# A layer-norm, state-space and MLP kernel on one core: one ScalarE table set loaded by name, and a skip term moved from diagonal matmuls to elementwise ops

## Chip, cores and metric

One core of a Trainium2 chip. The metric is device time in microseconds (us) of one execution; lower is better. The profiled execution has a span (first to last instruction), which is 1.7 to 2.1 us shorter than the device time.

A run more than 1.5% above the fastest run of the same kernel is called slow and left out of ratios. A ratio is the mean time of a kernel's fast runs over the mean of the fast runs of the kernel before in the same rounds, so it is not quite the ratio of the medians that are quoted beside it.

## The reference, cut to what matters

```python
xn = layernorm(x)                                  # x: 2048 tokens of 448
s  = 2*Re(C h) + xn*Dskip                          # h: complex recurrence over the tokens
g  = silu(gelu(layernorm(xn) @ w1 + b1) @ w2 + b2) # 448 -> 1792 -> 448
out = x + s*g
```

The kernel works on 4 groups of 512 tokens, each two blocks of 256, and splits a block into even and odd tokens ("par" 0 and 1). The recurrence runs on pairs of tokens. Even tokens get `xn*Dskip` inside a precomputed matrix M0. For odd tokens the skip term is the subject of half of this change.

## The kernel before

Every operation is a task with an engine, the data it reads and writes, and a place in a fixed list, `ORDER`. That list was made beforehand by a planner. Each engine runs its tasks strictly in that order. Some tasks can run on either of two engines; `SECOND` lists those that take their second choice.

The parts that matter:

```python
# a warming activation: it makes ScalarE load a table set early
act(lambda e: e.activation(sgn[0:1, 3:4], sgn[0:1, 2:3], ACT.Ln, scale=-1.0), ["sgn"], ["warm"], ...)
...
ld("pool", b2bc[:], dram_ap(B_b2, 0, [[0, 128], [1, D]]), ["b2bc"], ..., reads=["sgn3"])   # sgn3 waits for "warm"
...
def first_norm():            # the first 128 even and 128 odd tokens, ahead of everything
    for par in range(2):
        ... bn_stats, bn_aggr on VectorE
        kb.add("act", [lambda e: e.activation(r1, var, ACT.Ln, ...),
                       lambda e: e.activation(r1, r1, ACT.Exp, scale=-0.5)], ..., chain=True)   # 1/sqrt(var)
        ... scale on VectorE, transpose on PE, copy on VectorE
...
def mm1_half(j, b, k3, prio):  # x @ w1 for one block of group 0: 8 matmuls, then gelu on ScalarE
    ...                        # needs the half (or both halves) of w1 that its columns lie in
...
def ym(g, b, par, prio):       # the output of one tile of 128 tokens
    ... 7 matmuls of h against CZ or CQ
    if par == 0: ... 4 matmuls xnT x M0
    else:        # odd tokens: xn * Dskip as matmuls against diagonal matrices Do
        fns += [lambda e: e.matmul(psum[:, bk, a:z], xnT[:, gx, 3 + i, xs], Do[:, i, ...], start=False, ...) for i, a, z in cuts]
    dve: t3 = psum * g_sb ;  dve: o_sb = t3 + x
```

## Time and profile before

| | before |
|---|---|
| device time, median | 165.68 us |
| first dense matmul (`mm1_half`, line L694) | 10.48 us |
| end of `mm1_half`, start of `mm2` | 25.67 us |
| PE idle from then to the last M0 matmul, which ends at 158.98 | 0 |
| table loads on ScalarE | 10 |

The page of the profile gives busy time, share of the span and instructions of each engine. Then come the granted PE clock in 40 equal slices (a digit is tenths of full speed) and the engines on the chain that ended last, that is, on the chain of work and waits that leads to the last instruction. PE is TensorE's matmuls and PEld its weight loads; DVE is VectorE, ACT ScalarE, POOL GpSimd; SP (SyncE) issues most transfers. A q behind a name means the queue that issues for that engine.

```profile
PE 155.3 (95%) x977; PEld 100.3 (61%) x977; DVE 124.5 (76%) x251; ACT 98.8 (60%) x156; POOL 33.4 (20%) x115
...
PEclk9955999999999999999999999999999999999999
...
PE 91%; ACT 3%; DVE 2%; DMA 1%; issue 1%; DVEq 0%
```

PE, the matmul engine, is the bound. The two fives in the clock row are a stretch at half speed. It begins at 8.82 and ends at 15.65 us, just where the dense matmuls start.

The timeline shows the head. Columns are start, duration, engine, source line, operation, output<-input, shape, count, and in brackets the idle time before it with what ended it.

```profile
3.81 0.29 ACT L368 ACTIVATE lnw<-lnmv,eps 128x1 f32<-128x1 f32 x1
4.12 1.28 ACT L369 ACT_TABLE_LOAD   x1
...
5.41 0.20 ACT L369 ACTIVATE lnw<-lnw 128x1 f32<-128x1 f32 x1
...
5.63 1.28 ACT L368 ACT_TABLE_LOAD   x1
...
6.93 0.29 ACT L368 ACTIVATE lnw<-lnmv,eps 128x1 f32<-128x1 f32 x1
...
7.24 1.28 ACT L369 ACT_TABLE_LOAD   x1
...
8.54 0.20 ACT L369 ACTIVATE lnw<-lnw 128x1 f32<-128x1 f32 x1
...
9.31 0.61 PE L374 MATMUL psum<-ident,xn_sb 128*128 128x128 bf16 x4 [2.81 <-DVE xn_sb L371]
...
10.48 7.04 PE L694 MATMUL psum<-xn2T,w_sb 128*128 128x256 bf16 x40 [0.56 <-issue]
```

Ln and Exp alternate, and each finds the other's table set loaded. Three loads of 1.28 us lie in series before the first dense matmul, and PE waits 2.81 us for them. The 40 matmuls that follow take 7.04 us because most of them run at half clock.

The second half of w1 is also on its way.

Issued at 3.7 and 4.2, w1's second half is complete at 12.06. Before, PE gets that far only at about 15.6, so it hurts nobody.

The diagonal matmuls show on the chain of waits (start, duration, what):

```profile
93.77 0.20 PE psum L739 x4
```

### The profile page before, as it was taken

What the parts mean: (1) busy time and instruction counts of PE and PEld (TensorE: products, weight loads), DVE (VectorE), ACT (ScalarE), POOL (GpSimd) and SP (SyncE); (2) the same over time, 40 slices, a digit from 0 to 9 for tenths busy, and PEclk for the clock granted to TensorE, in tenths of its full rate; (3) what the DMA queues carried; (4) which work ended last, traced back from release to release, by engine and by line L of the source; (5) the groups of instructions that cost most, each with busy time, mean ns of one, the idle gap of its engine ahead of it and who ended that gap; (6) DMA issues with size and microseconds to landing.
All of it is one profiled execution on the core that took longest, in us unless ns stands there. A gap on an engine that the chain in (4) does not pass through costs nothing.

```text
span 164.2 us, 2747 instructions
## 1 busy us (share of the span) xinstructions
PE 155.3 (95%) x977; PEld 100.3 (61%) x977; DVE 124.5 (76%) x251; ACT 98.8 (60%) x156; POOL 33.4 (20%) x115
## 2 busy tenths in 40 slices
PE   5559999999999999999999999999999999999991
PEld 5447996566766765555555555566667675555560
DVE  5175798976499988899996969732499489988953
ACT  4997979987958599965544480452158953360200
POOL 5227795400000580000205420000002300000000
PEclk9955999999999999999999999999999999999999
DMA  4999966899874006400000056402050000010021
GB/s 93 341 273 390 242 68 139 181 166 176 165 147 116 0 0 126 113 4 0 0 0 0 2 127 116 112 0 56 4 168 0 0 4 0 0 58 0 31 85 58
DMA packets 29880, 14.61 MB, mean 89 GB/s; under 512 B 24581, under 2 KB 29577, under 8 KB 29866
## 3 DMA queue, kind: packets, MB, share of 16 engines
q1 hardware_dynamic: 29810, 14.31, 37.2%
q0 software_dynamic: 48, 0.11, 0.5%
q8 instruction: 8, 0.13, 0.3%
q14 instruction: 6, 0.05, 0.1%
q10 hardware_dynamic: 8, 0.00, 0.0%
HBM read 6.77 MB, written 1.84 MB: 52 GB/s over the span
## 4 chain that ended last, share of the span: by engine, by line
PE 91%; ACT 3%; DVE 2%; DMA 1%; issue 1%; DVEq 0%
PE psum L709 26%; PE psum L678 22%; PE psum L608 13%; PE psum L730 12%; PE psum L694 9%; PE psum L733 4%; PE psum L597 3%; ACT L369 2%; DMA x_all<-in_A_x_dram 1%; PE psum L739 1%; DVE t L743 1%; ACT L368 1%; DVE tmp L745 1%; DVE lnst L366 0%; PE psum L374 0%
## 5 line engine op out<-in xcount | busy, mean ns | idle before, releaser
L709 PE MATMUL psum<-w_sb,gT 128*128 128x448 bf16 x224 | 44.2, 352 | 0.0
L678 PE MATMUL psum<-xn2T,w_sb 128*128 128x512 bf16 x168 | 38.6, 379 | 0.0
L709 PEld LDWEIGHTS psum<-w_sb,gT 128*128 128x128 bf16 x224 | 21.8, 98 | 19.3
L685 ACT ACTIVATE gT<-psum 128x1024 bf16<-128x1024 f32 x21 | 21.5, 1023 | 15.0 <-PE psum L678 13.3
L678 PEld LDWEIGHTS psum<-xn2T,w_sb 128*128 128x128 bf16 x168 | 21.6, 132 | 12.5 <-issue 0.2
L608 PE MATMUL psum<-xnT,BT 128*128 128x256 bf16 x196 | 24.0, 273 | 0.0
L608 PEld LDWEIGHTS psum<-xnT,BT 128*128 128x128 bf16 x196 | 19.0, 98 | 4.7 <-issue 0.3
L743 DVE TENSOR_TENSOR t<-psum,g_sb 128x448 bf16<-128x448 f32 (+2 forms) x17 | 10.1, 594 | 10.7 <-PE psum L733 8.6
L713 ACT ACTIVATE th<-o 128x448 f32<-128x448 f32 x16 | 8.8, 571 | 11.9 <-DVE o L712 11.8
L694 PE MATMUL psum<-xn2T,w_sb 128*128 128x256 bf16 x112 | 15.1, 304 | 0.6 <-issue 0.6
L633 DVE TENSOR_TENSOR_SCAN s_f<-cw,cur,v_sb 128x256 f32<-128x256 f32 x21 | 14.7, 735 | 0.3
L694 PEld LDWEIGHTS psum<-xn2T,w_sb 128*128 128x128 bf16 x112 | 13.3, 137 | 2.1 <-issue 0.8
L712 DVE TENSOR_TENSOR o<-psum,b2bc 128x448 f32<-128x448 f32 x16 | 9.8, 622 | 4.8 <-PE psum L709 4.7
L612 ACT ACTIVATE u_sb<-psum 128x512 bf16<-128x512 f32 x12 | 7.1, 595 | 9.9 <-PE psum L608 9.9
L730 PE MATMUL psum<-CQ,h_sb 128*128 128x448 bf16 (+2 forms) x63 | 12.0, 332 | 0.0
L730 PE MATMUL psum<-CZ,h_sb 128*128 128x448 bf16 x56 | 11.9, 352 | 0.0
L417 ACT ACTIVATE xn_sb<-x_all,lnw 128x448 bf16<-128x448 bf16 x16 | 11.4, 749 | 0.1
L714 DVE SCALAR_TENSOR_TENSOR g_sb<-th,o 128x448 bf16<-128x448 f32 x16 | 9.8, 619 | 1.8 <-ACT th L713 1.7
L701 ACT ACTIVATE gT<-psum 128x512 bf16<-128x512 f32 x14 | 8.2, 592 | 1.9 <-PE psum L694 1.7
L730 PEld LDWEIGHTS psum<-CQ,h_sb 128*128 128x128 bf16 x63 | 6.0, 98 | 4.2
L352 DVE BATCH_NORM_STATS2 lnst<-x_all 128x6 f32<-128x448 bf16 x14 | 8.3, 603 | 0.0
L730 PEld LDWEIGHTS psum<-CZ,h_sb 128*128 128x128 bf16 x56 | 5.4, 98 | 4.6
(151 smaller groups left out, 197.0 us busy)
## 6 DMA issues: line engine op xcount, KB each, us to landing
w_sb<-in_B_w_dram SPq DMA_DIRECT2D x2, 784.0 KB, 9.5
out_dram<-tmp SPq DMA_DIRECT2D x7, 224.0 KB, 2.2
w_sb<-in_B_w_dram SPq DMA_DIRECT2D x2, 672.0 KB, 6.2
x_all<-in_A_x_dram SPq DMA_DIRECT2D x3, 448.0 KB, 3.8
gT<-in_A_C_re_dram SPq DMA_DIRECT2D x1, 392.0 KB, 12.6
Bn<-in_A_B_re_dram SPq DMA_DIRECT2D x1, 336.0 KB, 8.3
Bn<-in_A_B_im_dram SPq DMA_DIRECT2D x1, 336.0 KB, 8.3
gT<-in_A_C_im_dram SPq DMA_DIRECT2D x1, 336.0 KB, 3.7
```

What stands on the lines that cost most here:

```text
L417: ("act", lambda e: e.activation(dst, src, ACT.Identity, bias=nb, scale=rs), 0.75, 0.2)]
L608: fns = [lambda e, r=r, m=m, d=d: e.matmul(psum[:, 4, r * NK:(r + 1) * NK], BT[:, m, d, :], xnT[:, gx, d, :], start=(d == 0), stop=(d == 6 ...
L633: dve(lambda e, i=i, ri=ri, init=init: e.tensor_tensor_scan(s_f[:, i, ri, :], col(R2, i).to_broadcast([128, NK]), v_sb[:, i, ri, :], init, ...
L678: fns = [lambda e, k=k, d=d: e.matmul(psum[:, b0 + k, :], w1_sb[:, d, fcol(2 * j + k)], rhs[:, d, :, :], start=(d == 0), stop=(d == 3)) fo ...
L685: act(lambda e: e.activation(gT[:, gb, 2 * j:2 * j + 2, :], psum[:, b0:b0 + 2, :], ACT.Gelu_apprx_tanh), [f"ps{b0}", f"ps{b0 + 1}"] + (WK ...
L694: fns = [lambda e, k=k, d=d: e.matmul(psum[:, banks[k], :].rearrange("p (r c) -> p r c", r=2)[:, :, cs], w1_sb[:, d, fcol(2 * j + k)], rhs ...
L709: fns = [lambda e, fi=fi: e.matmul(psum[:, bk, 0:D], gT[:, gb, fi, q * 128:(q + 1) * 128], w2_sb[:, fi, :], start=(fi == 0), stop=(fi == N ...
L712: dve(lambda e: e.tensor_tensor(o2[:, fb, :], psum[:, bk, 0:D], b2bc[:], ALU.add), [f"ps{bk}", "b2bc"], [f"oo{fb}"], 0.62, prio - 76)
L713: act(lambda e: e.activation(th[:, fb, :], o2[:, fb, :], ACT.Tanh, scale=0.5), [f"oo{fb}"] + (WK + WKP if g == 0 else []), [f"th{fb}"], 0. ...
L714: dve(lambda e: e.scalar_tensor_tensor(out=g_sb[:, gs, :], in0=th[:, fb, :], scalar=1.0, in1=o2[:, fb, :], op0=ALU.add, op1=ALU.mult), [f" ...
L730: fns = [lambda e, k=k: e.matmul(psum[:, bk, c0:c1], h_sb[:, hb, k, k0:k0 + 128], cm[:, k, c0:c1], start=(k == 0), stop=False) for k in ra ...
L743: dve(lambda e: e.tensor_tensor(t3[:, fb, c0:c1], psum[:, bk, c0:c1], g_sb[:, gs, c0:c1], ALU.mult), [f"ps{bk}", f"g{gs}"], [f"t3{fb}_{c0} ...
```

## The change

Its intent is twofold. One load of the table set that holds both ln and exp should replace the loads between them. The skip of odd tokens should leave PE, the bound, for engines with idle time. The new residual `xr = x + g*(xn*Dskip/2)` takes three elementwise ops per odd tile, each on GpSimd or VectorE. (The g in it is the kernel's `g_sb`, which holds twice the g of the reference; hence the half.)

```diff
-            act(lambda e: e.activation(sgn[0:1, 3:4], sgn[0:1, 2:3], ACT.Ln, scale=-1.0), ["sgn"], ["warm"], 0.2, 4 * PINNED, "exp")
+            act(lambda e: e.preload_act_table_set("natural_log_exp_and_others"), [], ["warm"], 0.05, 5 * PINNED, "exp")
...
-            pool(lambda e: e.memset(sgn[:, 3:4], math.pi / 2), ["warm"], ["sgn3"], 0.1, S0)
+            pool(lambda e: e.memset(sgn[:, 3:4], math.pi / 2), ["sgn"], ["sgn3"], 0.1, S0)
...
             ld("pool", b2bc[:], dram_ap(B_b2, 0, [[0, 128], [1, D]]), ["b2bc"], 114688, -50, reads=["sgn3"])
+            ld("pool", dbc[:], dram_ap(A_Dskip, 0, [[0, 128], [1, D]]), ["dbc"], 114688, -20, reads=["b2bc"])
+            pool(lambda e: e.tensor_scalar(dbc[:], dbc[:], 0.5, None, op0=ALU.mult), ["dbc"], ["dbc"], 0.8, -20)
...
+            def skip(g, b, prio):
...
+                for o, i0, i1, op, rd, wr, d1 in ((xd[:, b, :], xn_sb[:, b, D:896], dbc[:], ALU.mult, [f"xn{b}", "dbc"], f"xd{b}", 0.35),
+                                                  (xr[:, b, :], xd[:, b, :], g_sb[:, gs, :], ALU.mult, [f"xd{b}", f"g{gs}"], f"xr{b}", 0.55),
+                                                  (xr[:, b, :], xo, xr[:, b, :], ALU.add, [f"xr{b}"] + xk(2 * g + b), f"xr{b}", 0.55)):
+                    kb.either(("pool", ...), ("dve", ...), rd, [wr], prio)
...
-                        fns += [lambda e, i=i, a=a, z=z: e.matmul(psum[:, bk, a:z], xnT[:, gx, 3 + i, xs], Do[...], ...) for i, a, z in cuts]
+                        fns[-1] = lambda e: e.matmul(psum[:, bk, c0:c1], h_sb[:, hb, 6, k0:k0 + 128], cm[:, 6, c0:c1], start=False, stop=True)
...
+                    res = xr[:, b, c0:c1] if par else x_all[:, 2 * g + b, 0, c0:c1]        # xr is f32
```

`ORDER` and `SECOND` were planned anew (cut here).

## The prediction

> What bounds the kernel now. The chain of waits is 91% PE: a head of 10.48 us, then PE without a gap until 158.99, then about 5 us of VectorE drain and last store. So only three things move the time: when the dense matmuls start and at which clock, how much PE work there is, and whether another engine becomes late.
>
> Head (timeline, chain). The first norm's Ln, Exp, Ln, Exp on ScalarE pays a table load of 1.28 us at 4.12, 5.63 and 7.24, all three on the chain. The Trainium skill ("ScalarE: Activation LUTs", table sets) says natural_log_exp_and_others holds both functions, and about 1283 ns per load; the trace shows 1283 ns. PE waits 2.8 us for this, and the windows view shows the granted clock at 0.5 from 8.8 to 15.65.
>
> After: one load, over before x lands (2.90 and 3.43). The second row is normalised at about 5.5; mm1 could start at 6.9. It then meets a new limit, the weights: the first half of w1 lands at 6.4 (its 64-row rest 7.05), the second at 11.5 (rest 12.06). So mm1 starts at 7.1 rather than 10.5, runs three groups (24 matmuls) to about 9.9, then waits for w1's second half until about 11.8. Clock: the cold stretch was two 3.41-us windows after a half idle one ("TensorE: Matmul & The Clock Gate", Part 1; the trace agrees: 0.5 for 6.8 us) and cost 2.5 us. With a shorter gap I expect none at first, but the wait for w1 may bring one cold window (1.7 us). The half-block mm1, now ending at 25.84, should end at 21.9 (warm) to 23.6 (one cold window): 2.2 to 3.9 us gained, not the 3.85 of the loads one for one.
>
> PE work. The diagonal matmuls are 0.20 us per odd tile, 8 tiles: 1.6 us, all on the chain.
>
> Moved and added. Of 24 tensor ops of 128x448 the order puts 9 on VectorE and 15 on GpSimd. By traced ops of that shape (0.39 bf16, 0.62 with f32) VectorE gets 4.8 us, and 1.7 from the final add reading f32; it loses 5 diagonal builds (1.2): 124.5 to about 129 us. GpSimd gets about 20 us (33 to 53), at an estimated 1.3 us each, with idle time to spare. ScalarE loses 5 loads. VectorE was 16.6 of 17 us busy between 71 and 88 us, so it is the likeliest new limit; I allow 0.8 us of new PE gaps. The last adds with f32 cost 0.1 us; their xr should be ready about 1.5 us ahead.
>
> Sum: 165.7 - 3.2 (head) - 1.6 + 0.8 + 0.1 = 161.8; as the order was planned anew, with transposes of B and C earlier, I shade it to 161.5 us, range 159.8 to 163.9. Chances: faster by over 2% 0.67, within 2% 0.31, slower 0.02.
>
> What would show it: table loads 10 to 5, none between Ln and Exp; mm1's first matmul at about 7.1; a PE gap of 1 to 2 us near 10 to 12 ended by the DMA of w1; cold clock for 0 or 3.4 us rather than 6.8; no Do matmuls; the chain about 91% PE still; VectorE about 129 us busy.
>
> What would make it wrong: a longer cold clock around the w1 wait, so that the head gains under 2; GpSimd and VectorE slowing each other, so that xr or h comes late and PE gets gaps from 70 to 110; GpSimd ops far above 1.3 us; or w1 landing earlier than before, 1 to 2 us more.

## More of the kernel before

In the view of DMA issues from 3.5 to 4.5 us the columns are the transfer, the issuing queue, the count, the size, and the time from issue to landing.

```profile
w_sb<-in_B_w_dram SPq DMA_DIRECT2D x1, 672.0 KB, 7.8
b2bc<-in_B_b_dram POOLq DMA_DIRECT2D x1, 112.0 KB, 6.4
w_sb<-in_B_w_dram SPq DMA_DIRECT2D x1, 112.0 KB, 7.9
```

## The result, and the profile after

| | before | after |
|---|---|---|
| device time, median | 165.68 us | 160.97 us |
| ratio, 95% interval | | 0.9719 (0.9703 to 0.9736) |
| first dense matmul | 10.48 | 7.45 |
| start of `mm2` | 25.67 | 20.80 |
| PE gaps after that | 0 | 0.95 us |
| end of the last M0 matmul | 158.98 | 153.93 |
| span | 164.2 | 159.4 |

The time fell within the range, 0.5 us below the forecast. Where it came from, in the spans: 4.87 us up to the start of `mm2` (25.67 - 20.80), 0.18 from there to the last M0 matmul (133.31 - 133.13), and 0.25 given back in the drain (5.22 to 5.47). That makes 4.80.

The page of the kernel after, the same three lines:

```profile
PE 151.2 (95%) x944; PEld 97.3 (61%) x944; DVE 132.8 (83%) x254; ACT 92.6 (58%) x152; POOL 56.6 (36%) x132
...
PEclk9999999999999999999999999999999999999999
...
PE 72%; DMA 10%; SPq 4%; DVE 4%; POOL 4%; ACT 2%; issue 1%; DVEq 0%; ACTq 0%; POOLq 0%
```

The cold stretch is gone. PE is still busy 95% of the span but holds only 72% of the chain: something else got in. The head, in the timeline:

```profile
2.16 1.28 ACT L283 ACT_TABLE_LOAD   x1 [2.16 <-issue]
...
3.85 0.29 ACT L373 ACTIVATE lnw<-lnmv,eps 128x1 f32<-128x1 f32 x1 [0.41 <-DVE lnmv L372]
4.18 0.20 ACT L374 ACTIVATE lnw<-lnw 128x1 f32<-128x1 f32 x1
...
4.52 0.29 ACT L373 ACTIVATE lnw<-lnmv,eps 128x1 f32<-128x1 f32 x1
...
4.85 0.20 ACT L374 ACTIVATE lnw<-lnw 128x1 f32<-128x1 f32 x1
...
7.45 2.80 PE L699 MATMUL psum<-xn2T,w_sb 128*128 128x256 bf16 x24 [1.22 <-DMA w_sb<-in_B_w_dram]
...
10.72 1.93 PE L699 MATMUL psum<-xn2T,w_sb 128*128 128x256 bf16 x16 [0.46 <-issue]
```

No load stands between Ln and Exp, and both rows are scaled 3.7 us sooner (4.85 against 8.54). The brackets now name the new limit: the first 24 matmuls wait for w1's first half. PE then stops for 0.46 us, until w1's second half has landed at 10.63. That half came 1.4 us sooner than before (view of DMA issues, kernel after, 3.5 to 4.5 us; b2's load is no longer in that view):

```profile
w_sb<-in_B_w_dram SPq DMA_DIRECT2D x1, 672.0 KB, 6.4
w_sb<-in_B_w_dram SPq DMA_DIRECT2D x1, 112.0 KB, 6.4
```

What took PE's share of the chain is in the chain of waits from 27 us on (start, duration, what):

```profile
27.00 3.99 DMA dbc<-in_A_Dskip_dram
...
31.08 1.49 POOL dbc L338
...
32.72 1.04 POOL xd L730
...
33.86 1.02 DVE xn_sb L421
...
34.91 0.55 ACT xn_sb L422
...
35.58 0.56 ACT th L718
36.14 0.49 ACT u_sb L617
...
36.87 1.70 PE psum L613 x14
```

`dbc`, the skip weights, is loaded only after b2 has landed and after GpSimd's norm work. It lands at 31.0 and is halved. The first `xd` then reads `xn_sb`, and the next group's norm can overwrite `xn_sb` only after that. That norm stands on VectorE and ScalarE in front of `th` and `u_sb`, and `u_sb` frees the PSUM bank that PE needs. The totals of that stretch (20 to 46 us, view of waits: who waited for whom, total us, times, longest):

```profile
POOL dbc L338 <- DMA dbc<-in_A_Dskip_dram: 3.4, 1, 3.4
...
DVE xn_sb L421 <- POOL xd L730: 1.3, 1, 1.3
...
PE psum L613 <- ACT u_sb L617: 1.0, 2, 0.5
```

### The profile page after: what moved, and what is told of

Read it like the earlier page. It is cut to its first block, busy times and chain, and to the rows that moved or that the text cites. A ratio compares the mean times of both kernels' runs of the same rounds, so it can differ in the third digit from the quotient of the medians.

```text
span 159.4 us, 2700 instructions
## 1 busy us (share of the span) xinstructions
PE 151.2 (95%) x944; PEld 97.3 (61%) x944; DVE 132.8 (83%) x254; ACT 92.6 (58%) x152; POOL 56.6 (36%) x132
## 3 DMA queue, kind: packets, MB, share of 16 engines
HBM read 6.89 MB, written 1.84 MB: 55 GB/s over the span
## 4 chain that ended last, share of the span: by engine, by line
PE 72%; DMA 10%; SPq 4%; DVE 4%; POOL 4%; ACT 2%; issue 1%; DVEq 0%; ACTq 0%; POOLq 0%
PE psum L683 21%; PE psum L714 20%; PE psum L613 12%; PE psum L746 12%; DMA x_all<-in_A_x_dram 7%; SPq L84 4%; PE psum L749 4%; PE psum L602 3%; DMA dbc<-in_A_Dskip_dram 3%; DVE lnst L357 1%; POOL lnw L400 1%; POOL dbc L338 1%; DVE t L755 1%; PE psum L752 1%; POOL xd L730 1%
## 5 line engine op out<-in xcount | busy, mean ns | idle before, releaser
L683 PE MATMUL psum<-xn2T,w_sb 128*128 128x512 bf16 x168 | 38.1, 379 | 0.0
L683 PEld LDWEIGHTS psum<-xn2T,w_sb 128*128 128x128 bf16 x168 | 21.8, 132 | 12.9 <-issue 0.2
L690 ACT ACTIVATE gT<-psum 128x1024 bf16<-128x1024 f32 x21 | 21.5, 1023 | 11.8 <-PE psum L683 11.6
L719 DVE SCALAR_TENSOR_TENSOR g_sb<-th,o 128x448 bf16<-128x448 f32 x16 | 10.9, 682 | 4.4 <-ACT th L718 4.4
L699 PE MATMUL psum<-xn2T,w_sb 128*128 128x256 bf16 x112 | 12.8, 273 | 1.7 <-DMA w_sb<-in_B_w_dram 1.2
L699 PEld LDWEIGHTS psum<-xn2T,w_sb 128*128 128x128 bf16 x112 | 12.1, 132 | 2.0 <-DMA w_sb<-in_B_b_dram 1.4
L730 POOL TENSOR_TENSOR xr<-xd,g_sb 128x448 f32<-128x448 bf16 x4 | 4.5, 1119 | 24.8 <-DVE g_sb L719 20.9
L421 DVE TENSOR_SCALAR xn_sb<-x_all,lnw 128x448 bf16<-128x448 bf16 x20 | 10.3, 531 | 2.0 <-POOL xd L730 1.3
L746 PE MATMUL psum<-CQ,h_sb 128*128 128x448 bf16 (+2 forms) x54 | 10.5, 332 | 0.0
L422 ACT ACTIVATE xn_sb<-x_all,lnw 128x448 bf16<-128x448 bf16 x10 | 7.5, 755 | 4.4 <-DVE xn_sb L421 3.4
```

The source lines that it names most:

```text
L421: on = [("dve", lambda e: e.tensor_scalar(dst, src, rs, nb, op0=ALU.mult, op1=ALU.add), 0.4, 0.12), ("act", lambda e: e.activation(dst, sr ...
L683: fns = [lambda e, k=k, d=d: e.matmul(psum[:, b0 + k, :], w1_sb[:, d, fcol(2 * j + k)], rhs[:, d, :, :], start=(d == 0), stop=(d == 3)) fo ...
L690: act(lambda e: e.activation(gT[:, gb, 2 * j:2 * j + 2, :], psum[:, b0:b0 + 2, :], ACT.Gelu_apprx_tanh), [f"ps{b0}", f"ps{b0 + 1}"] + (WK ...
L699: fns = [lambda e, k=k, d=d: e.matmul(psum[:, banks[k], :].rearrange("p (r c) -> p r c", r=2)[:, :, cs], w1_sb[:, d, fcol(2 * j + k)], rhs ...
L719: dve(lambda e: e.scalar_tensor_tensor(out=g_sb[:, gs, :], in0=th[:, fb, :], scalar=1.0, in1=o2[:, fb, :], op0=ALU.add, op1=ALU.mult), [f" ...
L746: fns = [lambda e, k=k: e.matmul(psum[:, bk, c0:c1], h_sb[:, hb, k, k0:k0 + 128], cm[:, k, c0:c1], start=(k == 0), stop=False) for k in ra ...
```

## The experiments

They ran in three sets, each on another chip and with its own 7 runs of the kernel before, to which its ratios refer. Every time in the table is a median of 4 runs. Results were correct except where a wrong result is announced.

| run | median us (range) | ratio to before (95%) | `mm2` starts | PE gaps after it |
|---|---|---|---|---|
| before | 165.68 (165.54 to 165.7) | | 25.67 | 0 |
| after | 160.97 (160.87 to 161.19) | 0.972 | 20.80 | 0.95 |
| set 1: tab_only | 164.19 (163.17 to 165.92, slow) | 0.992 (0.985 to 0.999) | 22.50 | 0.28 |
| tab_b2bc | 164.74 (163.56 to 165.49) | 0.995 (0.990 to 1.000) | 22.20 | 2.07 |
| nodiag_only (wrong result) | 164.35 (163.95 to 164.49) | 0.993 (0.991 to 0.995) | 25.75 | 0 |
| after_oldtab | 166.42 (166.37 to 167.07) | 1.007 (1.005 to 1.009) | 24.76 | 2.58 |
| set 2: after_again | 161.86 (161.52 to 162.53) | 0.979 (0.977 to 0.982) | 21.52 | 0.64 |
| after_b2bc_early | 165.84 (164.59 to 166.44) | 1.002 (0.997 to 1.008) | 25.43 | 0.52 |
| after_dbc_early | 160.62 (160.12 to 161.68) | 0.972 (0.968 to 0.976) | 22.28 | 0.13 |
| after_skip_tiny (wrong result) | 161.0 (160.61 to 161.42) | 0.974 (0.971 to 0.976) | 21.62 | 0.46 |
| set 3: after_control | 161.52 (160.63 to 164.03, slow) | 0.974 (0.970 to 0.978) | 20.44 | 1.84 |
| tab_b2bc_mid | 161.83 (161.21 to 162.67) | 0.978 (0.974 to 0.982) | 21.24 | 0 |
| after_skip_dve | 161.33 (160.03 to 164.11, slow) | 0.973 (0.965 to 0.981) | 20.38 | 0.90 |
| dbc_warm | 161.34 (160.8 to 161.71) | 0.974 (0.972 to 0.977) | 21.69 | 0 |

The last two columns come from the one profiled execution, which need not be the median one. That matters for the kernels with an early start. Gaps under 0.1 us are left out.

### tab_only: the table set alone, in the old order

```diff
 # kernel before
-act(lambda e: e.activation(sgn[0:1, 3:4], sgn[0:1, 2:3], ACT.Ln, scale=-1.0), ...)
+act(lambda e: e.preload_act_table_set("natural_log_exp_and_others"), [], ["warm"], ...)
```

> The kernel before with one edit, the warming Ln replaced by the load of the set that holds ln and exp. Theory (the head is worth its table loads, up to the next limit, which is w1's second half): the dense matmuls start at 7.3 to 7.5 us instead of 10.48, pause from about 10.2 until w1's second half lands at about 12, no cold clock or one window, the half-block mm1 ends at 22.2 to 23.9 instead of 25.84, time 162.0 to 163.7 us. Rival (the old order was planned for a late start, so the transposes of B, which landed at 30 to 31, take the gain back as PE gaps near 30): 164 us or more, with gaps there.

Timeline of PE, kernel tab_only:

```profile
7.73 2.83 PE L694 MATMUL psum<-xn2T,w_sb 128*128 128x256 bf16 x24 [0.63 <-DVE xn2T L376]
12.43 1.93 PE L694 MATMUL psum<-xn2T,w_sb 128*128 128x256 bf16 x16 [1.87 <-DMA w_sb<-in_B_w_dram]
```

The head did what the theory said: an early start, then a pause of 1.87 us until w1's second half had landed, at 12.34. The times fall into two groups: 163.17 and 163.19, then 165.2 and 165.92. The mean granted clock of the runs was 0.996 and 1.0 in the first group, 0.99 in both of the second. One 3.4-us window at half clock would lower the mean by 0.01 (an estimate: 1.7 of 162 us). The profile of after_b2bc_early, which has just one such window, shows a mean of 0.990. So the second group looks like the cold window that the prediction feared after the pause. No profile fell on such a run, so this is argued, not shown. Only the quicker two lie in the theory's range of 162.0 to 163.7. The ratio of 0.992 mixes the groups (165.2 counts as fast); the quicker two alone give 0.986. The old order made only 0.28 us of new gaps; the rival's gaps near 30 were not there.

### tab_b2bc: with b2's load behind the parameter work, in the old order

```diff
 # tab_only; ORDER: the task that loads b2bc moved behind GpSimd's last-but-two parameter ops
```

> The same, and the load of b2 is moved in GpSimd's order behind its parameter work, as in the changed kernel. Theory (b2's broadcast load on the early queues is what held w1's second half back to 12.06 before and its absence let it land at 10.63 after): w1's second half lands at about 10.6, mm1's pause shrinks to about 0.5 us, the half-block mm1 ends at about 20.8, time 1.2 to 1.5 us below the run with the table alone. Rival (w1 landed earlier for another reason): same as the run with the table alone within 0.3 us.

w1's second half landed at 10.62, as expected. The run still was no faster than tab_only, for two reasons that its profile shows. The clock came up only at 11.14 (the trace's first record of full clock), so the first groups of `mm1_half` ran cold: 40 matmuls took 6.09 us without a pause. And b2 now landed too late, at 27.84, for its first reader. View of waits, kernel tab_b2bc, 25 to 42 us:

```profile
DVE o L717 <- DMA b2bc<-in_B_b_dram: 3.7, 1, 3.7
```

VectorE was held 3.7 us, and PE got 2.07 us of gaps. The experiment confounded two things, so tab_b2bc_mid repeated it later.

### nodiag_only: the diagonal matmuls taken out, nothing in their place

```diff
 # kernel before, wrong result on purpose
-fns += [lambda e, i=i, a=a, z=z: e.matmul(psum[:, bk, a:z], xnT[...], Do[...], ...) for i, a, z in cuts]
+fns[-1] = lambda e: e.matmul(psum[:, bk, c0:c1], h_sb[:, hb, 6, ...], cm[:, 6, c0:c1], start=False, stop=True)
```

> The kernel before without the diagonal matmuls of the odd tokens and with nothing in their place: WRONG RESULT on purpose. Theory (PE is the bound throughout, so their 8 x 0.2 us come off one for one): 164.0 to 164.3 us, ratio about 0.990 to 0.992. Rival (they hide under weight loads or other waits): 165.2 us or more.

From the start of `mm2` to the last M0 matmul it took 131.91 us instead of 133.31: 1.40, which is seven tiles of 0.20. The eighth tile ends behind the last M0 matmul, where the chain has passed to VectorE, and its 0.2 gains nothing. In device time the gain was 1.1 us by the medians, 1.2 by the ratio. So PE is the bound, as the theory says, but the term was 1.2 to 1.4, not 1.6.

### after_oldtab: the changed kernel with the old warming

```diff
 # kernel after
-act(lambda e: e.preload_act_table_set("natural_log_exp_and_others"), [], ["warm"], ...)
+act(lambda e: e.activation(cwk[0:1, 0, 0:1], sgn[0:1, 0:1], ACT.Ln, scale=-1.0), ["sgn"], ["warm", "cwk", "cwk3"], ...)
```

> The changed kernel with the old way of warming (an Ln on ScalarE before the norm), so that the loads come back between Ln and Exp. Theory: the dense matmuls start at about 10.5 again, the clock goes cold for 6.8 us again, the half-block mm1 ends at about 25.8; the new PE gaps of 0.95 us near 36 to 41 vanish, because PE comes later to them; time 164.3 to 165.3 us. Rival (the new order and the GpSimd work carry a good part of the gain): below 163.5 us.

It was slower than expected, and slower than the kernel before. Two lines of the timeline of PE, kernel after_oldtab:

```profile
10.45 6.11 PE L699 MATMUL psum<-xn2T,w_sb 128*128 128x256 bf16 x40 [0.56 <-issue]
...
120.93 1.94 PE L683 MATMUL psum<-xn2T,w_sb 128*128 128x512 bf16 x8 [1.27 <-DMA xn2T<-xn_sb]
```

The start went back to 10.45. The new order could not use a late start: b2 landed at 29.87 and `dbc` at 34.12. PE had gaps of 1.31 us from 30 to 42, ended by VectorE and by the transposes of B and of the norm. It had another of 1.27 at 120, ended by a transpose that the queue issued late. So with the old warming the rest of the change, in this order, gains nothing and costs 0.7%. The profiled execution is the slowest of the four (167.07), and its clock was up only from 13.69.

### after_again and after_control: the changed kernel twice more

```diff
 # kernel after, unchanged
```

> The changed kernel once more, as the control of this set and to see whether its time depends on where the free-running clock windows fall, as two of the kernels before did (163.2 and 165.2 to 165.9 us of the same kernel). Theory (its pause before w1 is only 0.46 us, so no cold window comes of it): all runs within 160.7 to 161.4. Rival (the phase of the windows matters to it as well): some runs 1 to 2 us longer.

> The changed kernel as control of this set: 160.9 to 162.5 us, as in the two sets before; whatever it is, the other three of this set are read against it.

The medians were 161.86 and 161.52; after_again misses its theory (160.7 to 161.4). So the changed kernel varies by about 1 us between sets (and chips), where the kernel before stayed within 165.2 to 165.8 in all of them. w1's second half landed at 10.63, 11.20 and 10.12 in the three profiles. The gaps near 36 to 41 were 0.95, 0.64 and 1.84. One control run took 164.03 us at a mean clock of 0.989. An early start exposes the kernel to when w1 lands, and probably to the clock. That landing scatters by itself: in the ten profiles without b2's load beside it, it came between 10.06 and 11.97, in the four with it (before, nodiag_only, tab_only, after_b2bc_early) between 11.66 and 13.45. So part of the 1.4 us between the two profiles shown further up may be chance.

### after_b2bc_early: the changed kernel with b2 loaded early again

```diff
 # kernel after; ORDER: the task that loads b2bc moved up, right behind the memsets of sgn
```

> The changed kernel with one load moved: b2's broadcast is issued early by GpSimd, as before. Theory (this load on the early queues delays w1's second half by 1.4 us, and the pause that this makes can bring a cold window): w1's second half lands at about 12.0, PE pauses 1.9 us, mm2 starts at about 22.2 (warm) or 23.9 (one cold window) instead of 20.80, part of it given back because the PE gaps near 36 to 41 vanish: 161.3 to 161.8 us warm, about 163 us with a cold window. Rival (the load does not matter): 161.0 us.

Timeline of PE, kernel after_b2bc_early, and its clock row:

```profile
6.86 2.80 PE L703 MATMUL psum<-xn2T,w_sb 128*128 128x256 bf16 x24 [0.86 <-DMA w_sb<-in_B_w_dram]
13.70 3.05 PE L703 MATMUL psum<-xn2T,w_sb 128*128 128x256 bf16 x16 [4.04 <-DMA w_sb<-in_B_w_dram]
```

```profile
PEclk9997899999999999999999999999999999999999
```

It was worse than expected: w1's second half landed at 13.45, PE idled 4.04 us, and a cold window followed from 14.33 to 17.74. Moving one 112-KB load to an earlier place lost the whole gain (165.84). The run puts it even earlier than it was before: GpSimd issued it at 3.38, not 4.12, ahead of w1's second half, which SyncE then issued at 4.32 instead of 3.73. So 0.6 us of the delay is a later issue. The Trainium skill ("DMA: Bandwidth & Descriptors", arbitration) says that each DMA engine goes round between the queues that have work, a packet at a time. The case is in keeping with this, though no view here shows the turns: with b2's load on another queue beside it, the last part of w1's second half took 8.7 us from issue to landing, against 5.9 to 7.0 in the three profiles of the changed kernel.

### tab_b2bc_mid: table set and b2's load out of the way, all else as before

```diff
 # tab_only; ORDER: the task that loads b2bc moved to the middle of GpSimd's parameter work (lands at 21.46)
```

> The kernel before with the named table set, and the load of b2 issued by GpSimd in the middle of its parameter work, so that it neither runs beside w1's load nor lands after its first reader (27.84, too late, in the run that put it behind all of that work). Old order, old diagonals. Theory (the head's gain needs both, the table set and b2's load out of the way of w1, and the old order can use it): w1's second half at 10.6 to 11.2, pause 0.5 to 1 us, mm2 starts at 20.8 to 21.6 where the clock is warm, PE gaps after it below 0.6, 161.5 to 163 us. Rival (the old order takes the gain back whatever the head does): 164 us or more with over 1.5 us of PE gaps between 25 and 45.

Timeline of PE, kernel tab_b2bc_mid:

```profile
7.60 2.80 PE L699 MATMUL psum<-xn2T,w_sb 128*128 128x256 bf16 x24 [1.02 <-DMA w_sb<-in_B_w_dram]
11.16 1.93 PE L699 MATMUL psum<-xn2T,w_sb 128*128 128x256 bf16 x16 [0.77 <-DMA w_sb<-in_B_w_dram]
```

The kernel before, with its old order, its diagonal matmuls and no skip ops, gets a ratio of 0.978 from these two edits. The full change in the same set has 0.974, and the intervals overlap. PE had no gap at all after the start of `mm2` (133.33 us to the last M0 matmul, against 133.31 before). The head carries most of the gain: by the means of this set 3.6 of 4.3 us. Skip ops and new order together add about 0.4% (161.22 over 161.88, means of the fast runs of this set), which this set doesn't resolve.

### after_dbc_early: the skip weights loaded sooner

```diff
 # kernel after
-ld("pool", dbc[:], dram_ap(A_Dskip, ...), ["dbc"], 114688, -20, reads=["b2bc"])
+ld("pool", dbc[:], dram_ap(A_Dskip, ...), ["dbc"], 114688, -20, reads=["sgn3"])
 # ORDER: this load moved right behind that of b2bc
```

> The changed kernel with the load of the skip weights issued by GpSimd directly behind that of b2, without waiting for b2 to land, so about 6 us sooner; nothing else moves. Theory (the chain load of dbc, its halving, xd, xn_sb, xn_sb on ScalarE, th, u_sb is what makes the two PE gaps of 0.95 us near 36 to 41): dbc lands at 24 to 25 instead of 31.0, both gaps vanish, 160.0 us, ratio to the changed kernel about 0.994. Rival (ScalarE's own work, with its table load at 37.3, makes the gaps): 160.8 us or more, gaps stay.

`dbc` landed at 25.5 instead of 31.9 (after_again's profile), and the gaps fell to 0.13 us. Against after_again, in the same set, the means of the fast runs are 160.76 and 161.95 us, a factor of 0.993; the intervals of the two ratios to before do not overlap. PE came to that stretch 0.76 us later than in after_again, which alone would shrink the gaps. But dbc_warm, with the same early load and `mm2` at 21.69, had no gap there either, and after_skip_dve, with the late load and no skip op on GpSimd, kept 0.90 us. So the late load is the cause of the gaps. In this set the version is 0.7% faster than the changed kernel. That is 1.2 us, more than the 0.5 us of gaps that went; where the rest comes from is not shown. Its profiled execution is also the slowest of its four (161.68), and the timeline shows why:

```profile
7.56 4.28 PE L703 MATMUL psum<-xn2T,w_sb 128*128 128x256 bf16 x24 [0.52 <-DVE xn2T L385]
```

The same 24 matmuls took 4.28 us instead of 2.80, because the clock came up only at 10.61. The warming matmuls (36 products of the identity matrix, from 1.4 us on, whose results nobody uses) are the same instructions as in the changed kernel.

### after_skip_tiny: the skip ops cut to one column

```diff
 # kernel after, wrong result on purpose
+o, i0, i1 = o[:, 0:1], i0[:, 0:1], i1[:, 0:1]      # all 24 skip ops and the halving of dbc
-res = xr[:, b, c0:c1] if par else x_all[:, 2 * g + b, 0, c0:c1]
+res = x_all[:, 2 * g + b, par, c0:c1]
```

> The changed kernel with all 24 skip ops and the halving cut to one column, in their places and with their waits, and the last adds reading x in bf16: WRONG RESULT on purpose. It shows what the added elementwise work costs. Theory (it costs the 0.95 us of PE gaps and 0.2 us of tail, and the rest is hidden): about 159.8 us, with VectorE's mean per op back to those of before (xn_sb from 0.53 to 0.40, h's second product from 1.16 to 0.95) since GpSimd no longer works beside it, VectorE busy about 124 us. Rival (contention costs more than the gaps show): 159.2 us or less. Other rival (nothing): 160.9.

It was 0.95 us faster than after_again (means 161.01 and 161.95), so the added elementwise work costs about 0.95 us. The theory put this down to the gaps and the tail; the two profiles, 0.5 us apart in span, don't show that: the gaps went from 0.64 to 0.46 (a wait for a transpose is left), the drain from 5.41 to 5.25, and PE's stretch without its gaps from 132.38 to 132.10. How the 0.95 divides is open. The groups of the profile show what else it does. Columns: line, engine, op, tiles and shapes, count | busy us, mean ns | idle before. The kernels are before, after, and after_skip_tiny:

```profile
L416 DVE TENSOR_SCALAR xn_sb<-x_all,lnw 128x448 bf16<-128x448 bf16 x14 | 5.3, 395 | 0.3 <-POOL lnw L397 0.2
```

```profile
L421 DVE TENSOR_SCALAR xn_sb<-x_all,lnw 128x448 bf16<-128x448 bf16 x20 | 10.3, 531 | 2.0 <-POOL xd L730 1.3 <-POOL lnw L402 0.4
```

```profile
L421 DVE TENSOR_SCALAR xn_sb<-x_all,lnw 128x448 bf16<-128x448 bf16 x20 | 7.5, 393 | 1.6 <-ACT xn_sb L422 0.8 <-POOL lnw L402 0.4
```

The same op takes 395 ns, 531 ns beside GpSimd's tensor ops, and 393 ns when those are tiny. The Trainium skill ("GPSIMD Engine Reference", Specifications) says that GpSimd shares its SBUF interfaces with VectorE and contends with ops in a two-port mode or with two SBUF inputs. The trace agrees that the two slow each other; it doesn't show the port mode. One such op took 1.02 us (33.86 in the chain above) while GpSimd was at the next `xd`.

### after_skip_dve: all skip ops on VectorE

```diff
 # kernel after; SECOND: all 24 skip tasks take their second engine, VectorE
```

> The changed kernel with all 24 skip ops on VectorE, in their places in the order; GpSimd keeps only the halving of dbc. Theory (GpSimd's tensor ops slow those of VectorE that run beside them, so GpSimd's help is worth less than the 15 ops it takes): VectorE's xn_sb op back to about 0.40 us, VectorE busy 132 to 135 us in all, about what it is with GpSimd's help, and the time within 0.7 us of the control. Rival (GpSimd's help is worth its 15 ops, VectorE becomes the bound): VectorE busy 138 us or more, time 1.5 us or more over the control.

VectorE was busy 134.2 us, against 132.9 in the control, although it took 15 more ops; its `xn_sb` op was back at 393 ns. The means of the fast runs are 160.90 and 161.22, no difference that these runs resolve (160.03 to 162.07). GpSimd's help bought VectorE about 1.3 us of busy time and no device time that shows.

### dbc_warm: PE kept busy while it waits for w1

```diff
 # after_dbc_early
+for bank, n in ((3, 12), (6, 8)):      # placed before the first and before the fourth group of mm1_half
+    pe([lambda e: e.matmul(psum[:, bank, 0:128], ident[:, :], ident[:, :], start=True, stop=True) for _ in range(n)], [], [f"keep{bank}"], ...)
```

> A candidate to beat both: the changed kernel with the early load of the skip weights (0.7% better in the set before) and two groups of matmuls into unused banks, 12 before the first dense group and 8 before the fourth, to keep PE busy while it waits for w1. Theory (the spread of 1 to 2 us between executions is the free-running clock window: where none was full of work before the dense matmuls start, these run cold until the next one ends): the clock is up by 8.5 us in any execution, the runs lie within 0.8 us, median 159.8 to 160.3, ratio to the control 0.985 to 0.992. Rival (the spread is w1's landing, not the clock): no better than the run with the early load, 160.6, and as wide.

The runs lay within 0.9 us and none was slow. But the median, 161.34, missed the forecast (159.8 to 160.3) and was no better than the control's 161.52 (means of the fast runs 161.30 and 161.22), and after_dbc_early itself was not in this set. So whether filler matmuls help is open, and this candidate is no gain over after_dbc_early as measured.

## Why the prediction was right, point by point

- **What bounds the kernel.** Right: PE without gaps before, and each us that PE started earlier came through.
- **Head, mechanism.** Right: 10 table loads became 5, none of them between Ln and Exp; a start at 7.45 (forecast 7.1), w1 as the next limit, a pause, and no cold stretch. The Trainium skill's statement ("ScalarE: Activation LUTs", table sets) that one set holds both functions is borne out by the run.
- **Head, size.** Mis-sized: 3.2 us was entered, and 4.87 came. The term that was off is w1's landing. The prediction carried it over from the kernel before ("the second at 11.5 (rest 12.06)") and let PE wait "until about 11.8"; moving b2's load out of the early traffic does not appear in its sum, and an earlier landing only among what would make it wrong. In the run w1's second half landed at 10.63, so the pause was 0.46 us instead of 1.9 and no cold window followed. tab_only, with b2's load still early, is the head as forecast: w1 at 12.34, a pause of 1.87, `mm2` 3.17 us sooner than before. With b2's load early, the changed kernel lost its whole gain (after_b2bc_early); with it moved away from w1, the old order got most of the gain (tab_b2bc_mid against tab_only).
- **Diagonal matmuls.** "1.6 us, all on the chain": 1.40 in the profile and 1.1 to 1.2 in time (nodiag_only), because the last tile's are behind the end of the PE chain.
- **New gaps.** The size was right (0.8 forecast, 0.95 found), the cause wrong. The prediction named VectorE, nearly full from 71 to 88 us. No gap appeared there. The gaps came at 36 to 41 from the late load of the skip weights, shown by after_dbc_early.
- **VectorE busy.** 132.8 us, not 129: the ops themselves were as forecast, but GpSimd's slowed their neighbours, the risk that the prediction had named. GpSimd's 15 ops took 1.12 to 1.26 us each in the mean of their kinds, about 18 us in all, near the forecast of about 20.
- **The chain "about 91% PE still".** Wrong: 72%, since the chain passes through that load.
- **Drain.** 0.1 forecast, 0.25 found: the last two adds with f32 took 0.43 and 0.36 us instead of 0.29 and 0.26.
- **The rest.** 1.40 saved and 0.95 lost should leave 0.45 between the start of `mm2` and the last M0 matmul; 0.18 was found. After gaps are taken off, the runs with the new order need 0.1 to 0.5 us more there (after_oldtab 0.7) than nodiag_only's 131.91. Where, is open.

So the total came near partly by luck. The head gained 1.7 us more than entered; a smaller diagonal term, slightly larger gaps, a longer drain and the untraced rest took back about 0.8 of it. The shading by 0.3 for the new order brought the forecast nearer to the result, but no run shows that the new order earned it. The total doesn't prove the split.

## What to carry to other kernels

When a change lets an engine start earlier, ask which transfer it will meet next and what else is in the DMA queues at that time: here one 112-KB broadcast beside the weights decided whether a table-set fix was worth 0.8% (1.4% in its quicker runs) or 2.2%. Moving work off the bound engine pays only if its operands arrive in time: the skip weights' late load gave back 0.95 of the 1.40 us that the diagonal matmuls had cost. And before giving tensor ops to GpSimd, count what they do to VectorE's ops running beside them.

## What the Trainium skill lacked or had wrong

- "ScalarE: Activation LUTs", *What ACT_TABLE_LOAD costs*: it gives 1283 ns for the load and about 1380 ns of drain besides, 2.66 us a switch. The load is 1.28 us here, but from the end of Ln (4.10) to the start of Exp (5.41) only 1.31 us pass, so no such drain shows.
- "TensorE: Matmul & The Clock Gate", Part 1: it lets the clock drop after an idle window. Before, it dropped at 8.82 after a window from 5.41 in which PE had worked until 6.50. The busy share below which the clock drops is not given. In the profiles here half clock followed windows with 0.63, 0.91 and 1.03 us of PE work (after_b2bc_early, nodiag_only, before), and not one with 1.54 (tab_only, 10.01 to 13.43).
- The same part says that under sustained activity the transition comes at around 4 us and varies by about 0.5 from run to run. The work before the dense matmuls isn't sustained here: warming matmuls from 1.4 or 1.8 us on for 3.2 us, then pieces. The first record of full clock came at 5.23, 5.41, 6.54, 10.61, 11.14 and 13.69 us in different profiles, and the late ones cost real time (24 matmuls 4.28 instead of 2.80 us). The page's figure doesn't carry over to such a head. The clock changes lie 3.41 us or a multiple of it apart, at another offset from the kernel's start in each profile. No page says that the clock row shows full speed before the first record, as it does in these.
- "GPSIMD Engine Reference": it names the contention with VectorE but gives no size ("SBUF — State Buffer" has the rule of who waits for whom and two factors of slowdown, no times for ops of this shape). Here VectorE's `xn_sb` op went from 395 to 531 ns in the mean, and one took 1.02 us. It gives tensor_tensor times at 2048 elements only; at 448 they were 1.12 to 1.26 us.
- "DMA: Bandwidth & Descriptors": it says queues interleave; no page puts a size on what a small broadcast does to a large load beside it. Here the last part of w1's second half took 7.5 to 8.7 us from issue to landing in the four profiles with b2's 112 KB beside it, and 5.9 to 7.8 in the ten without.
